# Expert number and reload condition held in registers between two weight transfers, and one weight set queued ahead of a slot's rows

## The chip, the core and the metric

One NeuronCore of a Trainium2 chip. The metric is the device time of one execution in microseconds. Engines in the profile's names: PE is TensorE's matmuls, PEld its weight loads, DVE is VectorE, ACT ScalarE, POOL GpSimd, SP SyncE. A name with q (SPq) is the engine's instruction queue itself, where register reads, waits and the issuing of DMA transfers are seen.

## The reference, cut to what matters

First an attention with squared ReLU, whose result is multiplied by u; then a mixture of experts in which each of the 19,968 rows goes to the one expert of 8 that fits it best.

```python
# attention: B, S, D = 8, 2496, 256; d_qk = 64
scores = (1.0 / S) * np.matmul(z, z.transpose(0, 2, 1))
out = u * np.matmul(np.maximum(scores, 0.0) ** 2, v)
# experts: N = 19968 rows x, E = 8, F = 1024
expert_idx = np.argmax(xn @ en.T / tau, axis=1)      # rows and embeddings normalized
for e in range(E):
    mask = expert_idx == e
    h = np.maximum(x[mask] @ w1[e], 0.0)
    out[mask] = gate_w[mask, None] * (h @ w2[e])     # gate_w: softmax value of that expert
```

Which row goes to which expert is known only at run time.

## The kernel before, in words

**Attention half.** Steps over batch, group of 512 columns and tile of 128 rows multiply z by z (lines 266 and 267), square the result and multiply it by v (306 to 308). After each group, `route` takes the finished rows, finds their expert and place, and GpSimd scatters them (line 458, four scatters per group, one after the other) into a DRAM buffer `xs` in which each expert has its own region. Beside this the weights of all experts are split into two fp16 parts and written to the DRAM buffer `wsd` (1 MB for w1, 1 MB for w2 of each expert).

**Expert half.** The rows of `xs` are worked through in slots, each of rows of one expert. The first 61 slots have 256 rows (table A), the next 41 have 128 (table B); the last 4 of these run only if they are needed, inside a branch (line 1018). For each slot k there are

- `slot_x` (lines 797 to 809): SyncE reads the slot's row offset into a register (line 800), issues a transposing load of the rows (807) and a load of their gates and row numbers (`me`, `mer`; 808). Eight buffers in turn hold them; a buffer is free when the output scatter of the slot eight before has landed.
- `slot_w(k, 0)` and `slot_w(k, 1)` (811 to 819): SyncE issues the transfer of the expert's w1 part (index 0, 1 MB) and w2 part (index 1). The expert number is read from the table into a register first (813, a tensor load, register arithmetic and a range check). There are four weight buffers in turn (`NWB = 4`). From slot 4 on a second read (818) gets a condition: whether the expert differs from that of the slot four before, which used the same buffer. The transfer at line 819 is issued with this condition and moves data only if it is 1. The slots are dealt out so that each buffer keeps one expert over long runs.
- `slot_up(k)` (821 to 844): 96 or 48 matmuls into chunks of PSUM (lines 836 to 838, tiles `ph`, three buffers), with a ReLU on ScalarE (840) and a remainder on VectorE (841) per chunk. This needs the rows and weight part 0.
- `slot_down(k)` (846 to 869): matmuls 860 to 862 into `po`, scaling on VectorE (866), and GpSimd's scatter of the output rows (867). This needs weight part 1.

I call the first multiplication of a slot its ups and the second its downs.

**What sets the order.** TensorE, VectorE, ScalarE and GpSimd get their order from the scheduler; SyncE's is written by hand, as its instructions stand in the code (line 874). `slot_first` is placed half a group before the attention ends and issues the loads of slot 0, both weight parts of slot 0, part 0 of slot 1, and the rows of slots 1 and 2. After the attention, at lines 986 to 995, the memory of the attention's tiles is given to the remaining weight buffers and row buffers, and part 1 of slot 1, then rows 3, weights 2, rows 4, weights 3, and rows 5 are issued. Then `work` (997 to 1012) issues per slot k: the rows of slot k + 6, the ups of slot k, part 0 of slot k + 4, the downs of slot k - 1, part 1 of slot k + 3.

The route steps of the last group, the computing of table B and `pads` (779 to 782, eight writes that pad each expert's region, issued by SyncE) are popped from a queue piece by piece during the first three slots.

Of the kernel before, what the change touches and what calls it, by code (L numbers as in the profile page):

```python
# [27 lines left out]
NWB = 4  # L28
# [15 lines left out]
def relu2_attention_then_moe(ctx, tc, zT, uT, v, emb, tau, w1, w2, ident, tri, iota_e, out):  # L44
    nc = tc.nc
    B, DQ, S = zT.shape
    D = uT.shape[1]
    E, _, F = w1.shape
# [738 lines left out]
    mst = {}  # L787
# [6 lines left out]
    def slot_of(k):  # L794
        return (tables["A"], k, TA) if k < KA else (tables["B"], k - KA, TB)

    def slot_x(k):

        tab, i, T = slot_of(k)
        off = nc.sync.value_load(tab[0:1, 0, i:i + 1], min_val=0, max_val=E * CAP + TB - T)  # L800
        if k < XFIRST:
            xt = mx.tile([P, 4, T], F16, name="xt16", tag="xt16")
            me = mx.tile([P, T // P, ROW - D], F32, name="me", tag="me")
        else:
            xt = mst["mr"].tile([P, 4, T], F16, name="xr16", tag="xr16")
            me = mst["mr"].tile([P, T // P, ROW - D], F32, name="mer", tag="mer")
        nc.sync.dma_start_transpose(xt, xs[bass.ds(off, T), :].bitcast(F16)[:, 0:2 * D])
        nc.sync.dma_start(me, xs[bass.ds(off, T), D:ROW].rearrange("(j p) w -> p j w", p=P))
        mst["x", k] = xt, me

    def slot_w(k, i):
        tab, c, _ = slot_of(k)
        e = nc.sync.value_load(tab[0:1, 1, c:c + 1], min_val=0, max_val=E - 1)
        src = wsd[bass.ds(e, 1), :, (0, WR1)[i]:(WR1, WR1 + WR2)[i]].rearrange("e p w -> (e p) w")
        if k < NWB:
            nc.sync.dma_start(mst["w"][i][k], src)
        else:
            new = nc.sync.value_load(tab[0:1, 2, c:c + 1], min_val=0, max_val=1)
            nc.sync.dma_start(mst["w"][i][k % NWB], src, cond=new, cond_hint=False)

    def slot_up(k):
# [50 lines left out]
    def slot_first():  # L872

        ctx.enter_context(tc.manual_schedule(engines={mybir.EngineType.SP}))
        mst["w"] = ([wp.tile([P, WR1], F16, name="wa0", tag="wr1"), wp.tile([P, WR1], F16, name="wa1", tag="wo")],
                    [wp.tile([P, WR2], F16, name="wb0", tag="wr2")])
        slot_x(0)
        slot_w(0, 0)
        slot_w(0, 1)
        slot_w(1, 0)  # L880
        for k in range(1, XFIRST):
            slot_x(k)
# [105 lines left out]
    slot_pools()  # L988
    slot_w(1, 1)
    for k in range(2, NWB):  # L990
        slot_x(k + 1)
        slot_w(k, 0)
        slot_w(k, 1)
    for k in range(NWB + 1, XAHEAD):
        slot_x(k)

# [93 lines left out]
```

## Time and profile before

| | us |
|---|---|
| median of 3 runs | 2234.69 |
| lowest and highest of them | 2231.22 and 2242.39 |
| the profiled execution | 2237.35 |
| its span, from the first to the last instruction | 2235.5 |

TensorE's mean granted clock in the profiled execution is 0.987 of full speed. The attention half lasts until about 1346 us in the span, when the first slot's ups begin. In the stretch from 1400 to 1900 us TensorE is busy without a gap; from 2000 to 2100 it is busy for 89.85 of 100 us and from 2100 to 2200 for 91.46. DMA engines are busy for less than half of these stretches (0.49 and 0.42).

How to read it: an engine's idle time matters only where the engine ends the chain. A wait names the engine and line that waited, what it waited for, the time in all, how many times and the longest. A group of instructions gives its count and the least, median and greatest duration in ns. A row of the timeline is the start in us from the span's start, the time in us, the engine, line, operation and tiles, and in brackets the idle time before it and who ended it.

### The profile page before, as it was taken

The numbers are of one execution on the slowest core, as the hardware profiler recorded it, in microseconds if no ns is written. First come the engines' busy times: TensorE is split into PE (matmuls) and PEld (weight loads), VectorE is DVE, ScalarE is ACT, GpSimd is POOL, SyncE is SP. The second block draws the span as 40 slices with busy tenths as digits, with TensorE's granted clock in tenths as the row PEclk, the third lists the DMA queues.
The fourth block names the chain that finished last, engine by engine and source line by source line (L and its number), as shares of the span: only waits on it lengthen the run. The fifth ranks groups of instructions, "written<-read, shape, count | busy, mean of one in ns | idle before, by whom it ended". The sixth has DMA issues, their size and how long they took to land. (4 is left out here: it accounts for less than half of the span.)

```text
span 2235.5 us, 43505 instructions
## 1 busy us (share of the span) xinstructions
PE 2156.4 (96%) x15114; PEld 1419.9 (64%) x15114; DVE 1414.7 (63%) x4293; ACT 1090.1 (49%) x2193; POOL 348.0 (16%) x428
## 2 busy tenths in 40 slices
PE   6999999999999999999999999999999999998986
PEld 2444545444445444545454457888888888898886
DVE  8788889788698788888788655333333333333322
ACT  7577667667567577666676632222222222221111
POOL 0011111111111111111111111211111111111111
PEclk9999999999999999999999999999999999999998
DMA  8858666766847758677665536432233422155343
GB/s 205 186 122 202 153 176 152 185 149 146 219 107 197 172 138 199 148 188 149 146 144 111 101 99 192 118 75 56 70 86 97 100 53 56 44 181 128 83 113 103
DMA packets 523569, 299.00 MB, mean 134 GB/s; under 512 B 443973, under 2 KB 486478, under 8 KB 515920
## 3 DMA queue, kind: packets, MB, share of 16 engines
q1 hardware_dynamic: 508160, 254.93, 49.5%
q0 software_dynamic: 15184, 41.24, 5.4%
q8 instruction: 121, 1.98, 0.4%
q14 instruction: 104, 0.85, 0.1%
HBM read 297.95 MB, written 59.60 MB: 160 GB/s over the span
## 5 line engine op out<-in xcount | busy, mean ns | idle before, releaser
L269 ACT ACTIVATE a<-sc 128x512 f32<-128x512 f32 (+1 forms) x480 | 282.6, 589 | 178.5 <-PE sc L267 141.2
L270 ACT ACTIVATE a<-a 128x512 f32<-128x512 f32 (+1 forms) x480 | 300.0, 625 | 13.2
L308 PEld LDWEIGHTS <-vv 128*128 128x128 f16 x1520 | 148.6, 98 | 178.6 <-DVE vv L252 6.0
L860 PE MATMUL po<-w,hh 128*128 128x256 f16 x944 | 257.3, 273 | 0.6 <-ACT hh L840 0.6
L862 PE MATMUL po<-w,hl 128*128 128x256 f16 x944 | 257.3, 273 | 0.0
L861 PE MATMUL po<-w,hh 128*128 128x256 f16 x944 | 257.3, 273 | 0.0
L307 PEld LDWEIGHTS <-vv 128*128 128x128 f16 x1520 | 149.0, 98 | 168.6 <-issue 11.3
L867 POOL DMA_INDIRECT out_dram<-ot,mer x153 | 148.7, 972 | 663.7 <-DVE ot L866 432.5
L306 PEld LDWEIGHTS <-vv 128*128 128x128 f16 x1520 | 149.0, 98 | 161.0 <-issue 1.7
L458 POOL DMA_INDIRECT xs<-row,dsti x160 | 169.1, 1057 | 477.1 <-DMA xs<-row,dsti 343.6
L306 PE MATMUL acc<-tt,vv 128*128 128x512 f16 (+1 forms) x640 | 236.5, 370 | 3.2 <-DVE xt L336 3.0
L308 PE MATMUL acc<-tt,vv 128*128 128x512 f16 (+1 forms) x640 | 236.3, 369 | 0.0
L307 PE MATMUL acc<-tt,vv 128*128 128x512 f16 (+1 forms) x640 | 236.3, 369 | 0.0
L266 PE MATMUL sc<-z 128*128 128x512 f16 (+1 forms) x480 | 183.0, 381 | 9.0 <-DVE z L190 4.7
L866 DVE TENSOR_SCALAR ot<-po,mer,w 128x256 f32<-128x256 f32 x114 | 58.0, 540 | 206.3 <-PE po L862 202.4
L267 PE MATMUL sc<-z,z 128*128 128x512 f16 (+1 forms) x480 | 183.0, 381 | 0.0
L861 PEld LDWEIGHTS <-hh 128*128 128x128 f16 x1272 | 124.5, 98 | 14.7 <-issue 0.8
L862 PEld LDWEIGHTS <-hl 128*128 128x128 f16 x1272 | 124.5, 98 | 14.4
L860 PEld LDWEIGHTS <-hh 128*128 128x128 f16 x1272 | 124.5, 98 | 14.0
L360 ACT COPY x<-pm 128x256 f32<-128x256 f32 x160 | 58.5, 366 | 143.1 <-PE pm L343 141.0
L836 PEld LDWEIGHTS <-w 128*128 128x128 f16 x768 | 77.5, 101 | 27.9 <-DMA w<-wsd 21.9
L361 DVE COPY lg<-pm 128x8 f32<-128x8 f32 x160 | 25.6, 160 | 103.4 <-ACT x L360 101.8
(4160 smaller groups left out, 5343.7 us busy)
## 6 DMA issues: line engine op xcount, KB each, us to landing
w<-wsd SPq DMA_DIRECT2D x73, 1026.0 KB
wa<-wsd SPq DMA_DIRECT2D x50, 1024.0 KB
w<-wsd SPq DMA_DIRECT2D x48, 1024.0 KB
wb<-wsd SPq DMA_DIRECT2D x25, 1026.0 KB
scan<-in_v_dram SPq DMA_DIRECT2D x56, 312.0 KB
vt<-in_v_dram SPq DMA_DIRECT2D x133, 128.0 KB
ut<-in_uT_dram SPq DMA_DIRECT2D x32, 512.0 KB
wr<-in_w_dram SPq DMA_DIRECT2D x16, 1024.0 KB
```

Of the source, the lines that this page charges most:

```text
L266: nc.tensor.matmul(sc[:, :n], z1[:, ss], z1[:, t0:t0 + n], start=True, stop=False)
L267: nc.tensor.matmul(sc[:, :n], z1[:, ss], z2[:, t0:t0 + n], start=False, stop=True)
L269: state["at"] = nc.scalar.activation(a[:, :n], sc[:, :n], AF.Relu, scale=2.0 ** -SHIFT).ins
L270: nc.scalar.activation(a[:, :n], a[:, :n], AF.Square)
L306: nc.tensor.matmul(acc[k][:, :n], va, ph[:, :n], start=first, stop=False)
L307: nc.tensor.matmul(acc[k][:, :n], va, pl[:, :n], start=False, stop=False)
L308: nc.tensor.matmul(acc[k][:, :n], vb, ph[:, :n], start=False, stop=last)
L458: nc.gpsimd.indirect_dma_start(xs[:, :], bass.IndirectOffsetOnAxis(ap=loc["dsti"][:m, j:j + 1], axis=0), row[:m, j, :], None)
L860: nc.tensor.matmul(o, hh[:, f, t], wh, start=(f == 0), stop=False)
L861: nc.tensor.matmul(o, hh[:, f, t], wl, start=False, stop=False)
L862: nc.tensor.matmul(o, hl[:, f, t], wh, start=False, stop=(f == NF - 1))
L867: nc.gpsimd.indirect_dma_start(out, bass.IndirectOffsetOnAxis(ap=me.bitcast(U32)[:, j, 1:2], axis=0), ot[:, j, :], None, bounds_check=N - ...
```

## The change

The two parts touch `slot_w` and the order of the issues after the attention. In `slot_w`, expert number and condition are read in the call for part 0, kept in a dictionary, and taken from there in the call for part 1, so that they stay in registers from one to the other (one loop step of `work` lies between). In the order, weights 2 and rows 3 change places, and so do weights 3 and rows 4.

```diff
     def slot_w(k, i):
         tab, c, _ = slot_of(k)
-        e = nc.sync.value_load(tab[0:1, 1, c:c + 1], min_val=0, max_val=E - 1)
+        if i == 0:
+            e = nc.sync.value_load(tab[0:1, 1, c:c + 1], min_val=0, max_val=E - 1)
+            new = None if k < NWB else nc.sync.value_load(tab[0:1, 2, c:c + 1], min_val=0, max_val=1)
+            mst["e", k] = e, new
+        else:
+            e, new = mst.pop(("e", k))
         src = wsd[bass.ds(e, 1), :, (0, WR1)[i]:(WR1, WR1 + WR2)[i]].rearrange("e p w -> (e p) w")
-        if k < NWB:
+        if new is None:
             nc.sync.dma_start(mst["w"][i][k], src)
         else:
-            new = nc.sync.value_load(tab[0:1, 2, c:c + 1], min_val=0, max_val=1)
             nc.sync.dma_start(mst["w"][i][k % NWB], src, cond=new, cond_hint=False)
...
     slot_w(1, 1)
     for k in range(2, NWB):
-        slot_x(k + 1)
         slot_w(k, 0)
         slot_w(k, 1)
+        slot_x(k + 1)
```

## The prediction

> **What bounds the kernel now.** I read the page first, then the waits of TensorE in the expert half, then busy time by stretch, then the timeline and single lines of SyncE's queue, which issues every weight transfer.
>
> ```profile
> span 2235.5 us, 43505 instructions
> ...
> PE 2156.4 (96%)  x15114; PEld 1419.9 (64%)  x15114; DVE 1414.7 (63%) x4293; ACT 1090.1 (49%) x2193; POOL 348.0 (16%) x428
> ```
>
> TensorE (PE) is busy for 96% of the span, so the change can win only in TensorE's gaps and in what the gaps cause. The waits of PE from 1300 us on (engine and line, who ended the wait, us in total, times, longest):
>
> ```profile
> PE ph__17470 L836 <- DMA w<-wsd: 5.3, 1, 5.3
> PE ph__29031 L836 <- DMA w<-wsd: 5.0, 1, 5.0
> PE ph__29990 L836 <- DMA wa<-wsd: 4.5, 1, 4.5
> PE ph__31771 L836 <- DMA w<-wsd: 4.5, 1, 4.5
> PE ph__30812 L836 <- DMA w<-wsd: 4.0, 1, 4.0
> PE ph__32385 L836 <- DMA w<-wsd: 1.8, 1, 1.8
> ```
>
> All six are the first up-multiplication of a slot, waiting for its first weight half. By their times they belong to slots 2, 70, 77, 90, 83 and 95, counted from zero. What a stall costs in all is read from stretches that run from the moment when the slot's ups were due to the start of the next slot's ups. Columns: stretch, its length, busy time of PE, PEld, DVE, ACT and POOL with counts, granted clock, DMA share, GB/s.
>
> ```profile
> 1363.70:1381.87 18.17, 12.88 (x99) 10.54 (x98) 6.19 (x22) 2.62 (x5) 1.99 (x3) 0.81 1.01 291
> 1455.35:1507.75 52.40, 52.40 (x482) 46.98 (x480) 18.80 (x30) 11.94 (x20) 9.72 (x10) 1.00 0.32 77
> 2008.35:2034.85 26.50, 26.50 (x363) 25.15 (x360) 9.62 (x15) 5.97 (x10) 6.24 (x7) 1.00 0.35 94
> 2034.85:2212.30 177.45, 157.07 (x2018) 148.09 (x2016) 53.92 (x84) 33.43 (x56) 27.20 (x28) 0.94 0.47 123
> 2040.15:2052.66 12.51, 7.49 (x75) 7.05 (x74) 1.93 (x3) 1.19 (x2) 0.97 (x1) 0.73 0.77 229
> 2085.27:2096.84 11.57, 7.09 (x74) 6.68 (x73) 1.93 (x3) 1.19 (x2) 0.97 (x1) 0.85 0.69 209
> 2123.35:2134.42 11.07, 7.09 (x74) 6.66 (x73) 1.93 (x3) 1.19 (x2) 0.97 (x1) 0.85 0.65 200
> 2166.23:2178.55 12.32, 7.85 (x75) 7.43 (x74) 1.93 (x3) 1.19 (x2) 0.97 (x1) 0.72 0.74 202
> 2199.75:2207.01 7.26, 5.47 (x75) 5.05 (x74) 1.93 (x3) 1.19 (x2) 0.97 (x1) 1.00 0.66 233
> ```
>
> The second and third rows are clean stages of five slots each (ten ACT instructions over 256-row slots are twenty here, two per 128-row slot): 52.40 / 5 = 10.48 us for a slot of 256 rows, 26.50 / 5 = 5.30 us for one of 128. The first stall's slot took 18.17, so it lost 18.17 - 10.48 = 7.69 us; the gap is 5.3 of it, and the rest is the granted clock, 0.81 over the stretch. In the short-slot stage, the five bad slots lost 7.21, 6.27, 5.77, 7.02 and 1.96 us, 28.2 together. The fourth row says the same without picking: 28 slots (56 ACT, two each) took 177.45 where 28 x 5.30 = 148.4 were due, so 29.05 us are lost. The stalls of 4.0 us and more also lost clock; the one of 1.8 kept it at 1.00.
>
> Why are the weights late there? SyncE's waits from 2018 to 2206 us, all of them, and its row transposes, one per slot, in the same stretch:
>
> ```profile
> SPq L819 <- DVE hl L841: 0.4, 1, 0.4
> SPq L819 <- DMA w<-wsd: 0.2, 1, 0.2
> ```
>
> ```profile
> L807 SPq DMA_TRANSPOSE xr<-xs x29: 1222/1249/2307, 2018.3 to 2192.8; - x29
> ```
>
> SyncE waits 0.6 us out of 188: it is the bound itself. Its period is (2192.8 - 2018.3) / 28 = 6.23 us a slot, against TensorE's 5.30. So its lead melts by 0.9 us a slot, TensorE stops at the next slot whose expert differs and whose weights therefore really move, and each stop gives SyncE a new lead. For slot 70 the first half was issued here (row of the timeline: start, duration, two transfers merged):
>
> ```profile
> 2039.95 1.96 SPq L819 DMA_DIRECT2D w<-wsd  x2
> ```
>
> It was due at 2040.15, the start of the fifth stretch above, and the 5.0 us stall followed: from issue to use a reload takes about 5.4 us (0.2 of lead plus the wait and its end).
>
> **The change part by part.**
>
> *The reads that fall away.* For every slot from 4 on, the second weight transfer no longer reads expert and condition. Median durations of those reads (min/median/max in ns), half of these counts being the ones removed:
>
> ```profile
> L813 SPq TENSOR_LOAD <-Btab x63: 3/274/507, 2020.6 to 2205.2; - x63
> L813 SPq FUSED_REGOPS  x63: 13/164/171, 2020.9 to 2205.5; - x63
> ```
>
> ```profile
> L818 SPq TENSOR_LOAD <-Btab x63: 129/266/462, 2021.2 to 2205.8; - x63
> L818 SPq FUSED_REGOPS  x63: 111/153/169, 2021.5 to 2206.1; - x63
> ```
>
> ```profile
> 2034.14 0.07 SPq L819 DMA_DIRECT2D wa<-wsd  x1
> 2035.75 0.07 SPq L819 DMA_DIRECT2D wb<-wsd  x1
> ```
>
> The four add up to 0.274 + 0.164 + 0.266 + 0.153 = 0.86 us, the lower bound of the saving; the range checks and the small gaps between instructions come on top. The upper bound is the whole distance between the first and second transfer's issue, 2035.75 - 2034.14 = 1.61, of which the address sum and the issue itself stay. I take 1.15, somewhat under the middle for that reason. SyncE's slot becomes 6.23 - 1.15 = 5.08 us, below TensorE's 5.30; at the lower bound it is 5.37, a hair above. The Trainium skill (DMA: Bandwidth & Descriptors, Latency and other measured facts) puts the floor of a tensor_load at about 600 ns. The rows show 266 to 274, so the measurement decides; by the page the saving would be 0.66 larger, an estimate of 1.8, and the 0.6 us that I leave at slot 70 below would go too.
>
> *Slot 70 afterwards.* SyncE's last real wait before this stage ends ahead of 2018.3, and four second transfers (slots 65 to 68) lie between it and slot 70's issue. So the issue comes 4 x 1.15 = 4.6 us earlier, at 2035.35, and is usable at 2035.35 + 5.4 = 2040.75 against 2040.15: 0.6 us of stall stays. Slot 71 reloads right behind it; I allow 0.4. From there the lead of 5.4 grows by 0.22 a slot, so at slots 77, 83, 90 and 95 the weights are there. With 0.86 instead of 1.15, slot 70 has 0.2 + 3.4 = 3.6 of lead and stalls 1.8, and the later four stall about half a us each: 4 us in all. So the stage gets 29.05 - 1.0 = 28 us shorter, between 25 and 29. What is late next there is nothing on SyncE: its row loads wait for scatters of eight slots before, which is not among the waits quoted. In the stage of 256-row slots SyncE has twice the time, and the saving lies beside TensorE's work: zero.
>
> *The third weight set.* Now (the timeline of SyncE, contiguous):
>
> ```profile
> 1346.82 0.35 SPq L816 DMA_DIRECT2D w<-wsd  x1
> 1361.02 1.26 SPq L807 DMA_TRANSPOSE xr<-xs  x1
> 1362.48 0.42 SPq L808 DMA_DIRECT2D mer<-xs  x1
> 1363.70 1.50 SPq L816 DMA_DIRECT2D w<-wsd  x2
> ```
>
> SyncE stands at slot 3's transpose from 1347 until 1361.02, because the rows are being scattered to memory until then, and slot 2's two weight halves are queued behind it. They are issued at 1363.70, the very time at which TensorE wants them. Moved ahead of it, they go out at about 1348: the last transfer of slot 1, into a tile of the same pool that lies over the attention's memory, went at 1346.82, so the memory is free. At 5.4 us for the first half and as much again for the second they are in place by 1359. The 7.69 us go.
>
> What they are moved past: the transpose and row load of slot 3 (one engine queue, SyncE's), and beside them GpSimd's four scatters:
>
> ```profile
> 1349.28 0.96 POOL L458 DMA_INDIRECT xs<-row,dsti  x1 [11.69 <-DVE hl L841]
> 1352.87 0.96 POOL L458 DMA_INDIRECT xs<-row,dsti  x1 [2.62 <-DMA xs<-row,dsti]
> 1355.58 0.95 POOL L458 DMA_INDIRECT xs<-row,dsti  x1 [1.75 <-DMA xs<-row,dsti]
> ```
>
> The first, with slot 1's weights moving, took 3.59 us to the next; the second 2.71. With 2 MB more in flight the other three may each take 0.9 longer, so slot 3's rows come between 0 and 2.7 us later than 1361. The Trainium skill (DMA: Bandwidth & Descriptors, Queues, rings and completion order) has every DMA engine take turns between its queues packet by packet; the one pair of rows with and without weights agrees. By that rule all three scatters pay, the stall at slot 6 below is 3.4 instead of 1.5, and the end would be 2203. Slot 3 is due at 1363.70 + 10.48 = 1374.2, and its weights, issued by 1366 and landed by 1371.4, still make it. Slot 4's rows, put behind slot 3's weights, keep their place within 1 us and are due at 1384.7.
>
> *What the gap hid.* VectorE did the last routing steps during it:
>
> ```profile
> 1366.99 0.26 DVE L411 CAST ob<-oh 128x32 bf16<-128x32 f32 x1
> 1372.55 0.69 DVE L841 SCALAR_TENSOR_TENSOR hl<-ph__17470,hh 128x512 f16<-128x512 f32 x1 [5.30 <-ACT hh L840]
> ```
>
> Only from 1367.25 on can it take slot 2's first chunk, for 0.69 us, so its buffer is free at 1367.94. There are three such buffers and four chunks, each an eighth of the 10.48 us slot: TensorE's fourth chunk, due at 1363.70 + 3 x 1.31 = 1367.63, waits 0.3 us.
>
> *The next reload.* Slot 6's second half is real, and stands behind eight padding writes:
>
> ```profile
> 1413.22 8.45 SPq L782 DMA_DIRECT2D xs<-pad  x8
> 1423.39 0.18 SPq L819 DMA_DIRECT2D w<-wsd  x1
> ```
>
> ```profile
> 1429.15 0.27 PE L860 MATMUL po<-w,hh 128*128 128x256 f16 x1
> ```
>
> TensorE will want it 7.4 us sooner, at 1421.75. SyncE arrives sooner too: slot 2's pair of issues has left this stretch (2.3 us, from the end of the row load at 1362.90 to 1365.20), one read of slot 3 (half a pair, 0.57), and the pairs of slots 4, 5 and 6 (3.45): 6.3, less the 0 to 2.7 above. Issue 1417.1 to 1419.8, usable 1422.5 to 1425.2, stall 0.7 to 3.4 us. I take 1.5. Lost clock is the question at the upper end: the 1.8 us stall lost none, the 4.0 us one lost 5.77 - 4.0 = 1.8, so the end is 5.2.
>
> **Sum.** 29.05 - 1.0 + 7.69 - 0.3 - 1.5 = 33.9 us. The profiled execution took 2237.35 us (span 2235.5), 2.7 above the median of the runs, 2234.69; for it the sum gives 2203.4. I take the gain off the median, since nothing in the terms belongs to that one execution: 2234.69 - 33.9 = 2200.8, say 2201.
>
> **Rivals.** (a) *The first gain is given back at slot 6.* The padding writes wait for the last scatters; if these don't follow SyncE's earlier arrival, the writes still start at 1413.22, slot 6's half is issued 1.15 sooner at 1422.2, usable at 1427.6, and TensorE stalls 5.9 plus 1.8 of clock instead of 1.5: 6.2 us dearer, 2207. For it: the wait there is 13 us long and not SyncE's own. Against it: those scatters come behind slot loads that SyncE issues sooner. (b) *SyncE saves less than its reads.* If only 0.5 us a slot is won, its slot is 5.73, the lead still melts by 0.4 a slot, and of the 29 us some 13 remain: 2213. For it: transposes between 1.2 and 2.3 us show that other things stretch the period. Against it: the reads are in line, with no overlap in the rows. (c) *The reads don't go away*, because the held values are read again where they are used: only the ramp is won, 7.69 - 0.3 - 1.5 = 5.9, 2229. (d) *Slower: holding costs.* Two slots' values are alive at once on SyncE; if it had to store and re-read them, its slot would grow by as much as it should shrink, 6.23 + 1.15, and 28 slots lose 32 us more, less 5.9: 2261. It decides from 0.2 us added per slot on, since each added us costs 28. Nothing in the trace points to it: the address values held now cost nothing that it shows.
>
> **Numbers.** A difference under 0.5% (11 us) is about what a measurement of this kernel can't tell from no change. Chances: forecast 0.70, (a) 0.13, (b) 0.09, (c) 0.05, (d) 0.03. The range starts where no stall is left, 2234.69 - 36.7 = 2198, less 4 for the runs' own spread, 2194; it ends above (b), at 2215. Faster by over 0.5% (below 2223.5) are the forecast, (a) and (b): 0.92; within 0.5% is (c), 0.05; slower 0.03.
>
> **What would show it.** Right: from 2010 us on the transposes of SyncE come at 5.3 us or less and its waits for scatters reappear; 28 short slots take about 149.5; only a stall under 1 us at slot 70; slot 2's weights issued near 1348; a stall of 0.7 to 3.4 at slot 6's first down-multiplication, with no more than a short dip of the granted clock. Wrong: a SyncE period above 5.4 us with no waits, padding writes that don't start before 1413 relative to an unmoved end of the attention, or a new first stall at slot 3 for rows or weights.

## The result, and the profile after

The changed kernel takes 2203.53 us, the median of 4 runs (2199.26 to 2206.89); the kernel before, now with 4 runs as well, 2236.93 (2231.22 to 2242.39). The ratio is 0.985, with a 95% interval of 0.9815 to 0.9885: 33.4 us, or 1.5%, faster. The profiled execution took 2199.26 us, its span is 2197.5, 38.0 less than before's.

TensorE's waits from 1300 us on, after the change. The up-multiplications wait for no transfer any more; the only wait listed is slot 6's second weight half:

```profile
PE po L864 <- DMA w<-wsd: 1.9, 1, 1.9
```

The same kind of stretches as before the change (length, busy time of PE, PEld, DVE, ACT and POOL with counts, granted clock, DMA share, GB/s). The first is slot 2, the second runs from slot 7's ups to slot 8's with slot 6's downs between them, the third holds 28 short slots, from slot 69's ups to slot 97's:

```profile
1360.33:1371.08 10.75, 10.64 (x98) 9.39 (x96) 5.89 (x22) 2.40 (x5) 2.06 (x3) 1.00 0.73 239
1413.12:1425.69 12.57, 10.64 (x99) 9.38 (x96) 3.76 (x6) 2.39 (x4) 2.64 (x3) 1.00 0.69 168
```

```profile
2026.15:2174.55 148.40, 148.40 (x2019) 140.80 (x2017) 53.96 (x84) 33.44 (x56) 27.28 (x28) 1.00 0.60 143
```

Slot 2 takes 10.75 us where it took 18.17, 0.27 over a clean slot. Slot 6's late half costs 12.57 - 10.48 = 2.09. The 28 short slots take 148.40 us, which is 28 x 5.30 to the last digit: nothing is lost there, and PE is busy throughout at full clock. Before, the same slots took 177.45. The reason stands in SyncE's queue, the row transposes of the short stage:

```profile
L807 SPq DMA_TRANSPOSE xr<-xs x29: 1211/1227/2462, 2004.4 to 2147.4; - x29
```

29 of them in (2147.4 - 2004.4) = 143.0 us, 5.11 us a slot where it was 6.23, and below TensorE's 5.30. Now SyncE runs ahead. Slot 70's first half was issued here (both halves of two slots merged in one row), and its ups came at 2031.45, 8.2 us later; before the change the distance was 0.2:

```profile
2023.25 0.78 SPq L823 DMA_DIRECT2D w<-wsd  x2
```

Where the 38.0 us of the two profiles went: 29.05 are the short slots. The ramp, from slot 2 due to slot 12's ups, lost 7.81 us before and 2.48 now, which is 5.33. The end is 0.2 shorter. The other 3.4 can't be counted as the change's: the first ups began at 1342.74 instead of 1346.11, after an attention half of which the change touches only slot 0's loads at its end. In the eleven profiles of this study that moment lies between 1342.3 and 1349.4 us, and one and the same kernel, profiled twice, had it at 1343.4 and at 1348.1. So 34.6 us are the change's in the profile, 33.4 in the medians, 33.9 in the forecast. By its interval, the gain in the medians lies between 26 and 41 us: that forecast and measurement meet within half a microsecond is luck, and the terms are compared in the profiles below.

### The profile page after: what moved, and what is told of

It reads as the page before. It is cut to its first block, busy times and chain, and to the rows that moved or that the text cites. A ratio compares the mean times of both kernels' runs of the same rounds, so it can differ in the third digit from the quotient of the medians.

```text
span 2197.5 us, 42931 instructions
## 1 busy us (share of the span) xinstructions
PE 2142.2 (97%) x15114; PEld 1410.9 (64%) x15114; DVE 1414.9 (64%) x4293; ACT 1089.7 (50%) x2193; POOL 349.1 (16%) x428
## 5 line engine op out<-in xcount | busy, mean ns | idle before, releaser
L864 PE MATMUL po<-wb,hh 128*128 128x256 f16 x328 | 89.4, 273 | 0.0
```

Of the source, the lines that this page charges most:

```text
L864: nc.tensor.matmul(o, hh[:, f, t], wh, start=(f == 0), stop=False)
```

## The experiments

All ratios are to the kernel before, run beside them on the same chip.

### Each half of the change alone

The first keeps the shared reads and puts the order back:

```diff
     for k in range(2, NWB):
+        slot_x(k + 1)
         slot_w(k, 0)
         slot_w(k, 1)
-        slot_x(k + 1)
```

> The reads are shared as in the changed kernel, the order of weights 2 and 3 against rows 3 and 4 is that of before. Theory (SyncE's own instruction time bounds the short slots, and the reads were a sixth of it): SyncE's slot takes 5.1 us, the stalls at slots 70 to 95 are gone (29 us), the first stall of 5.3 us with its lost clock (7.7 us in all) stays, and slot 6 does not stall: about 2208 against 2237 for before. Rival (the order of the transfers did it, the reads lie beside other work): the stalls of the short slots stay, about 2232 to 2237.

Measured: 2208.51 us, ratio 0.9871 (0.985 to 0.9892). TensorE's waits, then the 28 short slots:

```profile
PE ph__17416 L840 <- DMA w<-wsd: 4.9, 1, 4.9
```

```profile
2033.09:2181.49 148.40, 148.40 (x2018) 140.78 (x2016) 53.98 (x84) 33.44 (x56) 27.19 (x28) 1.00 0.59 144
```

The stall at slot 2 stays, the short slots are clean without any change of order. The second has the new order and every read of before:

> The order of the changed kernel, with every read of before. Theory: the short slots are as before (6.2 us a slot on SyncE, 29 us lost); the first stall goes, but slot 6's second weight half, which comes behind all of SyncE's work, is 4 us later than in the changed kernel, so that a stall of 5 to 6 us, with clock 7, takes back what the first stall gave: 2233 to 2238, within 0.2% of before. Rival (the two parts add up by themselves): 5 to 6 us faster than before, 2231.

Measured: 2239.95 us, ratio 1.0001 (0.9988 to 1.0015). TensorE's waits:

```profile
PE ph__29990 L836 <- DMA wa<-wsd: 6.5, 1, 6.5
PE po L860 <- DMA w<-wsd: 5.9, 2, 4.9
PE ph__31771 L836 <- DMA w<-wsd: 4.8, 1, 4.8
PE ph__29031 L836 <- DMA w<-wsd: 3.9, 1, 3.9
PE ph__32385 L836 <- DMA w<-wsd: 2.3, 1, 2.3
PE ph__30812 L836 <- DMA w<-wsd: 0.7, 1, 0.7
```

No wait of slot 2 is among them, so the reordering did its work. But the second row holds 4.9 us at slot 6 (the other 1.0 is a short slot's), and the ramp up to slot 12 lost 7.68 us, against 7.81 before. What slot 2 gained, slot 6 took. By itself the order is worth nothing here; it needs the reads' saving to keep its gain. By the ratios the reads alone are worth 1.3%, the order alone nothing, both together 1.5%; the intervals of 1.3% and 1.5% overlap, so what the order adds is seen in the traces only. These give: the reads alone regain the 29.05 us of the short slots and nothing of the ramp (its loss up to slot 12 is 7.95 us), the order alone neither (7.68 us, and 27.97 in the short slots), both together 29.05 and 5.33.

### More and fewer reads

If SyncE's instruction time is the price, the loss must follow the number of reads. One kernel puts one read back into the changed kernel, so that a slot has three:

```diff
         else:
-            e, new = mst.pop(("e", k))
+            new = mst.pop(("e", k))[1]
+            e = nc.sync.value_load(tab[0:1, 1, c:c + 1], min_val=0, max_val=E - 1)
```

> The changed kernel with one of the two reads put back: the second transfer reads the expert number again and only the condition is shared. Theory: SyncE's slot takes 5.10 + 0.58 = 5.7 us, 0.4 more than TensorE's 5.30; the lead melts at less than half the former speed, stalls of 2 to 3 us come back at four or five of the slots 70, 77, 83, 90 and 95, 10 to 13 us in all with little lost clock: about 2214. Rival (a threshold: anything saved on SyncE is enough, since its row ring holds it back anyway): no stalls, 2203.

Measured: 2218.32 us, ratio 0.9907 (0.9886 to 0.9927). TensorE's two longest waits, at slot 6 (4.1 us of the first row) and at slot 77:

```profile
PE po L865 <- DMA w<-wsd: 5.1, 2, 4.1
PE ph__29306 L841 <- DMA wa<-wsd: 3.2, 1, 3.2
```

The other adds two reads to the kernel before, six a slot:

```diff
             new = nc.sync.value_load(tab[0:1, 2, c:c + 1], min_val=0, max_val=1)
+            if i == 1:
+                e = nc.sync.value_load(tab[0:1, 1, c:c + 1], min_val=0, max_val=E - 1)
+                new = nc.sync.value_load(tab[0:1, 2, c:c + 1], min_val=0, max_val=1)
+                src = wsd[bass.ds(e, 1), :, WR1:WR1 + WR2].rearrange("e p w -> (e p) w")
```

> The kernel before with the second transfer's two reads done twice, so that its slot has six reads instead of four. Theory: SyncE's short slot grows from 6.23 by 1.17 to 7.4 us, and 28 slots of it cost 2.1 us each over TensorE's 5.30, 59 us lost where before lost 29: 2266 to 2272. Rival (the reads lie beside other work, and what the changed kernel won came from holding values over the transfer): within 5 us of before, 2237 to 2243.

Measured: 2262.62 us, ratio 1.0124 (1.0099 to 1.0149), less than expected by 3 us. The row transposes and the 28 short slots, first with three reads, then with six:

```profile
L807 SPq DMA_TRANSPOSE xr<-xs x30: 1224/1233/2310, 2008.7 to 2172.8; - x30
```

```profile
2036.32:2192.44 156.12, 150.82 (x2019) 142.07 (x2016) 53.97 (x84) 33.44 (x56) 27.20 (x28) 0.99 0.56 139
```

```profile
L807 SPq DMA_TRANSPOSE xr<-xs x30: 1222/1232/1371, 2006.5 to 2216.1; - x30
```

```profile
2035.06:2236.61 201.55, 160.97 (x2019) 149.03 (x2017) 53.94 (x84) 33.43 (x56) 27.20 (x28) 0.93 0.41 109
```

| reads a slot | SyncE's period, us | (period - 5.30) x 28 | lost in 28 short slots |
|---|---|---|---|
| 6 | 7.23 | 54 | 53.15 |
| 4 (before) | 6.23 | 26 | 29.05 |
| 3 | 5.66 | 10 | 7.72 |
| 2 (changed) | 5.11 | 0 | 0.00 |

The period is the transposes' first to last start over 29 steps (28 for the changed kernel and the one before). The loss is about what SyncE's slot exceeds TensorE's by, times the slots, and zero once it is below. A pair of reads is 1.12 us between the changed kernel and the one before, 1.00 between before and six reads. The rivals of both kernels, a threshold and reads that lie beside other work, fall. The three-read kernel lost less in the short slots than expected (7.7, not 10 to 13), and in one stall of 3.2 us with small ones beside it, not in four or five of 2 to 3. Its slot 6 waited 4.1 us, which its expectation had left out; that half, too, is behind more reads.

### The wait at slot 6

The half that stalls slot 6 is issued behind the eight padding writes. Putting these one step later should free it:

```diff
-    queue += [table_b, pads]
+    queue += [table_b, lambda: None, pads]
```

> The changed kernel with the eight padding writes one step later, behind the second weight half of slot 6 instead of ahead of it. Theory: that half is issued some 20 us sooner (about 1392), the 1.9 us stall at slot 6 goes and nothing takes its place, no wait of TensorE over 0.2 us is left after the attention: 2 us, too little for the median. Rival: the padding writes hold up the loads of rows 10 and weights 8 behind them instead, and a stall of the same size comes at slot 8 or 10.

Measured: 2203.79 us, ratio 0.9848 (0.9828 to 0.9869). The rival was right. The half was issued at 1397.53, the stall at slot 6 was gone, and one of the same size stood at slot 8. TensorE's wait and SyncE's timeline:

```profile
PE ph__18545 L840 <- DMA wa<-wsd: 1.9, 1, 1.9
```

```profile
1412.81 1.40 SPq L807 DMA_TRANSPOSE xr<-xs  x1
1414.75 1.08 SPq L808 DMA_DIRECT2D mer<-xs  x1
1418.57 8.42 SPq L782 DMA_DIRECT2D xs<-pad  x8
1428.51 0.11 SPq L823 DMA_DIRECT2D wa<-wsd  x1
```

Rows 10 wait for the last scatters until 1412.81, the eight writes follow in a row, and slot 8's first half, which moves no data but has to be passed, is reached at 1428.51, behind slot 8's due time of 1426.64 (the end of slot 6's downs at 1426.80, less the usual overlap of 0.16). Popping the writes one at a time, so that SyncE's weights pass between them, was the next version:

```diff
-    def pads():
-        for e in range(E):
+    def pad_one(e):
+        def f():
             r = nc.sync.value_load(tails[0:1, e:e + 1], min_val=e * CAP, max_val=e * CAP + N)
             nc.sync.dma_start(xs[bass.ds(r, TB), :], pad[:TB])
+        return f
...
-    queue += [table_b, pads]
+    queue += [table_b, lambda: None] + [pad_one(e) for e in range(E)]
```

> The changed kernel with the padding writes behind slot 6's second weight half, and popped one at a time instead of eight together. Theory (the stalls at slots 6 and 8 came from SyncE's queue standing behind eight writes in a row): slot 8's first half is issued at most five writes behind rows 10, some 5 us ahead of its ups, and no wait of TensorE over 0.3 us is left after the attention: 2 us below the changed kernel, 2201, inside the noise of the median. Rival (the single writes each make a row load wait for their landing): SyncE falls behind by 2 us a slot and a stall comes at slots 8 to 11.

Measured: 2197.09 us, ratio 0.9832 (0.9811 to 0.9854), and TensorE has no wait left in the list after 1300 us. Ten slots from slot 2's ups on, first in the changed kernel, then here:

```profile
1360.33:1467.61 107.28, 105.25 (x968) 94.05 (x965) 44.45 (x108) 23.90 (x41) 23.44 (x25) 1.00 0.56 136
```

```profile
1360.97:1466.17 105.20, 105.09 (x968) 94.06 (x966) 44.31 (x108) 23.91 (x41) 23.43 (x25) 1.00 0.55 139
```

2.08 us less, as expected; ten clean slots are 104.8. The median fell by 6, three times that. But the two medians were not taken side by side, and the kernel before ran at 2235.24 beside this one and at 2236.93 beside the changed kernel. So the pair was run again, one beside the other.

> The changed kernel once more, beside the next one on the same chip. Theory: as before, one wait of about 2 us at slot 6 and none in the short slots; about 2203.

Measured: 2203.6 us, ratio 0.9848 (0.983 to 0.9865), with 2.0 us of wait at slot 6.

> The kernel with the padding writes spread, once more, to be compared with the changed kernel on the same chip. Theory (the 6 us by which it was faster in another call are 2 us of the stall at slot 6 and else chance): 2 us faster than the changed kernel. Rival (spreading the writes does something that the waits don't show): 5 to 7 us faster again.

Measured: 2200.51 us, ratio 0.9839 (0.9822 to 0.9856), 3 us below the changed kernel beside it. The two intervals overlap. That 2 us of stall are gone is seen in the traces; more than that is not shown. By its medians it is the fastest version here.

### What holds up the scatters

The forecast let each of the last three scatters of rows pay 0.9 us for the weights in flight. After the change they look like this:

```profile
1345.36 0.97 POOL L458 DMA_INDIRECT xs<-row,dsti  x1 [11.09 <-DMA me<-xs]
1352.79 0.96 POOL L458 DMA_INDIRECT xs<-row,dsti  x1 [6.46 <-DMA xs<-row,dsti]
1355.56 0.96 POOL L458 DMA_INDIRECT xs<-row,dsti  x1 [1.81 <-DMA xs<-row,dsti]
1358.30 1.18 POOL L458 DMA_INDIRECT xs<-row,dsti  x1 [1.78 <-DMA xs<-row,dsti]
```

One scatter took 7.43 us to the next, the others 2.77 and 2.74. The same three stretches (columns as above) show why only the first paid: SyncE had issued slot 1's second half and both halves of weights 2 from 1343.10 on, and most of these bytes moved during the first stretch.

```profile
1343.10 2.41 SPq L821 DMA_DIRECT2D w<-wsd  x3
1361.10 1.26 SPq L807 DMA_TRANSPOSE xr<-xs  x1
```

```profile
1345.36:1352.79 7.43, 7.43 (x70) 6.78 (x69) 3.55 (x8) 4.96 (x13) 0.96 (x1) 1.00 0.99 376
1352.79:1355.56 2.77, 2.77 (x28) 2.53 (x26) 1.14 (x4) 1.68 (x5) 0.96 (x1) 1.00 0.38 146
1355.56:1358.30 2.74, 2.74 (x28) 2.46 (x26) 2.67 (x16) 0.63 (x3) 0.96 (x1) 1.00 0.14 49
```

Is it the bytes in flight that slow the first one, or the transfers issued ahead of it? A kernel with only the first half of weights 2 moved ahead tells the two apart:

```diff
     for k in range(2, NWB):
         slot_w(k, 0)
-        slot_w(k, 1)
         slot_x(k + 1)
+        slot_w(k, 1)
```

> The changed kernel with only the first half of weights 2 (and 3) ahead of rows 3 (and 4); the second half comes behind them. Theory (a scatter's packets wait behind the weight transfers that were issued before it, one after the other, so only slot 1's second half and weights 2's first half hold it): the first of the four scatters still takes about 7.3 us to the next, rows 3 still come 18 us after the first slot's ups begin, and slot 6's stall stays at 2 to 3 us: 2203 to 2206. Rival (all bytes in flight share the engines, and the scatter is slow in proportion to them): 5 us or less for the first scatter, rows 3 two to three us sooner, slot 6 with at most a trace of a stall.

Measured: 2204.36 us, ratio 0.9866 (0.9842 to 0.9891). The scatters, and TensorE's waits:

```profile
1344.76 0.97 POOL L458 DMA_INDIRECT xs<-row,dsti  x1 [10.98 <-DMA me<-xs]
1352.29 0.96 POOL L458 DMA_INDIRECT xs<-row,dsti  x1 [6.56 <-DMA xs<-row,dsti]
```

```profile
PE po L864 <- DMA w<-wsd: 3.3, 1, 3.3
PE ph__17630 L840 <- DMA w<-wsd: 1.1, 1, 1.1
```

A third less data in flight, and the first scatter still takes 7.53 us, so its time doesn't follow the bytes in flight. With one transfer ahead it was 3.59 (before), 3.95 (the shared reads alone) and 3.27 (six reads). The second transfer costs it about 4 us more, the third nothing. That the order of issue decides this is not shown: in the changed kernel the third transfer, too, was issued just before the scatter, at 1345.17. By the trace's packet records the scatter's first data packet moved 4.4 us after its issue in the changed kernel and 4.6 in this one, 1.5 to 2.0 with one transfer ahead, 1.5 with none; what it stands behind stays open. Slot 6 waited 3.3 us, a little above the expected 2 to 3. Slot 3's first half, now behind rows 3 and one more half, was 1.1 us late, which neither theory had foreseen.

## Why the prediction was right, point by point

**The bound.** Right. SyncE's own instructions paced the short slots; its slot fell to 5.11 us, forecast 5.08. The price of 1.15 for a pair of reads measured 1.12 by the period. After the change 4.2 of the 143.0 us are SyncE's waits, 3.4 of them for scatters in three places (before, 0.6 of 174.5), so without waits the price is 1.25: the forecast lies between.

**Slot 70 afterwards.** The direction was right, the lead too small: 4.8 us forecast (0.2 and 4.6), 8.2 measured, so the 1.0 us that was to remain at slots 70 and 71 did not. The step that failed is "four second transfers lie between SyncE's last real wait and slot 70's issue": it took the stage before, where SyncE waits for scatters, as unmoved. Its waits for scatters there do not get shorter (28.9 us from 1950 to 2018 before, 30.5 from 1945 to 2010 after, six each), but they follow each other faster. The gate loads of rows 66 to 68 that end them, before and after:

```profile
1992.11 0.35 SPq L808 DMA_DIRECT2D mer<-xs  x1
...
2003.95 0.35 SPq L808 DMA_DIRECT2D mer<-xs  x1
...
2013.70 0.35 SPq L808 DMA_DIRECT2D mer<-xs  x1
```

```profile
1982.05 0.35 SPq L808 DMA_DIRECT2D mer<-xs  x1
...
1992.58 0.35 SPq L808 DMA_DIRECT2D mer<-xs  x1
...
2001.24 0.35 SPq L808 DMA_DIRECT2D mer<-xs  x1
```

From the last of them to slot 70's issue it took 26.25 us before and 22.01 after, so the four pairs of reads saved 4.2, near the forecast 4.6. The rest of the 8.2 comes from ahead of that point: the last gate load came 12.5 us sooner, slot 69's ups only 8.7, which makes 3.8 of lead that the forecast had put at nothing. The loads are 11.8 and 9.8 us apart before, 10.5 and 8.7 after, so each step is shorter by about the saving. That fits a chain in which the row load waits for a scatter, the scatter for the weights issued ahead of it, and the weights for SyncE's reads; the order in the chain is argued from these distances and was not tried by itself.

**The first stall.** Right: weights 2 are issued 2 us after the first ups, and slot 2 runs on time. Of the 7.69 us, VectorE's late routing steps keep 0.27 (forecast 0.3); in the second profile of the changed kernel TensorE waits 0.3 us there for VectorE's line 845.

**The scatters.** The step that failed is "with 2 MB more in flight the other three may each take 0.9 longer". The first scatter alone paid, 7.43 us against 3.59, and the cost came out above its range: rows 3 were issued at 1361.10, which is 18.4 us after the first ups against 14.9 before, so 3.5 later and not 0 to 2.7. Rows 4 came 2.9 later, not within 1; TensorE waited for neither. That the others took 2.77 and 2.74, as without weights, doesn't speak against the rule that the forecast took from the Trainium skill (DMA: Bandwidth & Descriptors, Queues, rings and completion order): nearly all of the weights had landed by then. The first scatter does speak against it, as far as one can see: its data did not take turns with two transfers from the start, its first packet moved 4.4 us after its issue, against 1.5 without weights.

**Slot 6.** Right in the result, by errors that partly cancel: the padding writes start at 1404.61 instead of 1413.22, the half goes out at 1414.17, and the stall is 1.9 us of wait (forecast 1.5, range 0.7 to 3.4) without lost clock:

```profile
1404.61 9.16 SPq L782 DMA_DIRECT2D xs<-pad  x8
1414.17 0.35 SPq L823 DMA_DIRECT2D w<-wsd  x1
```

Counted from the first ups, the half was issued 71.4 us after them instead of 77.3, so 5.9 sooner; the forecast's range was 3.6 to 6.3, and its stall of 1.5 meant 5.5. Of these, 3.9 stand in the loads ahead: rows 9, the last before the scatters that the padding writes wait for, were issued 45.4 us after the first ups (1388.10) instead of 49.3 (1395.36), where the reads and issues that left this stretch, less the scatters' 3.5, explain 1.7. The other 2 us were not traced to a cause. The term that was too small is the reload: from issue to use the half took 6.3 us (1414.17 to 1420.45), not the 5.4 of slot 70.

**Sum and rivals.** 33.9 us forecast, 33.4 measured. In the profiles the terms are 29.05 for the short slots (forecast 28.05), 7.42 for the first stall (7.39) and -2.09 for slot 6 (-1.5). Rival (a), the gain given back at slot 6, falls for this kernel, since the padding writes did follow SyncE's earlier arrival; without the reads' saving much of it happens: with the order alone the padding writes started 64.7 us after the first ups, only 2.4 sooner than before (61.9 in the changed kernel), and slot 6 waited 4.9 us. Rivals (b) and (c) fall with SyncE's period, (d) with it too: holding the values costs nothing that the period shows. The 600 ns that the Trainium skill (DMA: Bandwidth & Descriptors, Latency and other measured facts) gives as the floor of a tensor_load would have made a pair of reads dearer by 0.66, an estimate of 1.8 us; the measured 1.12 agrees with the rows' 266 to 274 ns.

## What to carry to other kernels

When weights arrive late, look at the issuing queue before the transfer: if it shows no waits, its own instructions are the bound, and each register read in it costs its full time in every slot (here about 0.55 us). Compare its period per unit of work with the bound engine's; the loss is about the difference times the count, and work below that line is free. A gain from moving one transfer ahead is kept only if what stands next in the same queue also comes sooner, so cost the next few transfers that really move data.

## What the runs showed of the hardware that had not been expected

A GpSimd scatter of 128 rows took 7.0 to 8.1 us to the next one where two or three weight transfers of 1 MB had just been issued (eight profiles), 3.3 to 4.0 behind one (three profiles), 2.7 to 2.9 with few or none in flight. The third transfer added nothing that stands out of this spread.

The length of a stall alone did not decide whether TensorE's granted clock fell. In the expert half all stalls of 3.2 us and more were followed by half clock, and none up to 1.95 us. Between these some were: 2.35 us (the order alone), 2.15 and 2.84 (six reads); 2.18 and 2.92 (both six reads) were not. In the attention half four stalls of 1.55 to 1.78 us, near 320 us, were followed by it. In each profile the stretches of half clock start at whole multiples of 3.41 us from one another, and all but the last, at the program's end, last one, two or three such steps. The stall of 2.15 us, from 2208.09 on, lies inside one step; that of 2.92, from 2223.08 on, is spread over two. Both with the step that follows (the granted clock is the third figure from the end):

```profile
2207.21:2210.62 3.41, 1.26 (x16) 0.92 (x14) 0.55 (x1) 0.00 (x0) 0.97 (x1) 1.00 0.66 257
2210.62:2214.04 3.42, 3.42 (x36) 3.42 (x34) 0.69 (x1) 0.60 (x1) 0.00 (x0) 0.50 0.29 57
2220.86:2224.27 3.41, 2.22 (x21) 1.75 (x18) 1.07 (x2) 0.00 (x0) 0.33 (x1) 1.00 0.73 274
2224.27:2227.69 3.42, 1.69 (x31) 1.70 (x32) 0.00 (x0) 0.14 (x1) 0.64 (x1) 1.00 0.13 48
2227.69:2231.10 3.41, 3.41 (x44) 3.17 (x42) 1.38 (x2) 1.05 (x2) 0.00 (x0) 1.00 0.87 291
```

The stall of 2.18 is spread over two steps as well. So it seems to be the idle share of a step that counts; that is read from these cases and no run tried it by itself.
